# Places of their own for the steps of an attention kernel's head, and other load orders around it

## The chip, the core and the metric

The kernel runs on one core of one Trainium2 chip. The metric is device time in microseconds (us) of one execution, the median of several. Engines are named as the profile names them: PE (TensorE, matmuls), PEld (its weight loads), DVE (VectorE), ACT (ScalarE), POOL (GpSimd), SP (SyncE, which issues almost all DMA transfers here).

## What is computed

Agent attention of four batches, followed by a feed-forward block with a maximum of three products ("maxout"). Cut to what matters:

```python
# q, k, v: (4, 12544, 128); agents: (4, 49, 128)
a2k     = softmax(scale * agents @ k.T)      # over the 12544 keys
agent_v = a2k @ v                            # (49, 128) for each batch
q2a     = softmax(scale * q @ agents.T)      # over the 49 agents
x       = (q2a @ agent_v).reshape(50176, 128)
h       = maximum(maximum(x @ w1, x @ w2), x @ w3)   # 768 columns
out     = h @ w_out                          # (50176, 128)
```

The softmax divides by the sum of exponentials, and the division can be put off to the very end, because the maximum of three linear maps scales with its input.

## The kernel before

**What it makes of the formulas.** For each batch the keys give 49 agent values, `av`. The kernel never forms x. It multiplies `av` by weight *differences* once for each batch: `wall` holds w2 - w1 (columns C21), w3 - w1 (columns C31; in block 4, `FI`, w3 - w2 instead) and linear columns (C1O: w1 times w_out, with zeros on both sides), and `G` is `av` times `wall`. Then for each group of queries: e = exp(scores); u = G[C31] times e, a = ReLU(u), v = G[C21] times e, r = max(v, a); the output is the linear part, e times G[C1O], plus the sum over six blocks of r times w_out, and last a scaling by 1/sum(e). In block 4 ReLU is applied to u in place, v is added onto it in PSUM, and ACT takes the second ReLU.

**Groups.** The 98 row tiles of 128 of a batch are cut into query groups of 8 (49 groups in all; the last takes the remainders of the four batches) and key groups of 9 (11 for a batch). A group has 6 blocks; each costs PE two matmuls for u and two for v (L662), ACT one 128x1024 ReLU (L677), DVE one 128x1024 maximum (L687), and PE eight output matmuls (L701). Two output halves are scaled by DVE (L708) and stored.

**Three parts.** In the head (function `head`) all keys and values of batch 0 are loaded and used, group by group, since G of batch 0 needs them all. In the body, each group of queries carries along one key group of the next batch (`k_group`), and at a batch's end `k_tail` makes the next G. The last batch's groups carry no keys.

**What sets the order.** Nothing is scheduled by dependencies: every step is recorded with a number by `at(key, fn)`, all are sorted by that number, and each engine executes its own steps in that order, waiting where data or a buffer isn't there yet. One query group is 6.0 units. The numbers come from tables: `KEY` for the steady state, `LATE` for groups of the last batch, `OWN` for groups 0, 1, 34 to 37, 47 and 48, `BORDER` for the groups around a change of batch, `BATCH0` and `BATCH3` for `k_tail`. A group's steps: `ld` load of queries, `qc` cast (POOL), `qt` turn (PE), `qe` copy out of PSUM (DVE), `s` scores (PE), `ex` exp (ACT), `sum` and `rec` sums and their reciprocals, `u0` to `u5`, `a0`, `v0`, `x0` and so on for the blocks (x is the maximum), `lin0`, `oc00` and so on for the output, `sc0`, `sc1` scaling, `st` store. Steps in the head have numbers counted from z, the place of the last key group, written as literals (lines 464 to 475).

**Queues and buffers.** All loads and stores stand in SP's one line. A load into the pool `loads` (14 buffers of 576 KB, tag st) is issued when its buffer is free and when the transfer eight before it has landed. PSUM has three buffers of two banks (tag uv) for turns, products and hidden blocks, and two of one bank (tag om) for scores, sums and outputs. Of `a_sb` there are three.

**Steps that the change and the prediction touch.** `load_w(i)` (line 264) loads w1, w2 or w3 as a whole; w1 and w3 are issued before the last values but one, query group 0 after these, w2 after the last values. `cast_w1` (ACT) and `turn_w1` (PE, then a DVE copy into `w1T`) prepare the linear columns. `differences_31`, `difference_f` and `differences_21` (lines 297 to 306) make `wall`; of w2 - w1 DVE takes the first 384 columns and POOL the other 384. `recip` and `normalise` make avT from the sums. `product(c0, on_vector)` (line 412) multiplies avT by 768 columns of `wall` into PSUM (L485) and copies them into G in two pieces, of 256 and 512 columns, on ACT (C31, L420) or DVE (C21, L418), directly after it. `warm(n)` issues n matmuls whose result isn't used (L328), twelve of them (`LAST_WARM`) after the last sums; `keep_busy` issues 32 such small matmuls, in pairs (L788), where groups -2 and -1 would have had their output matmuls. `load_w_out`, `cast_w_out`, `prep_linear` and `acc["lin"]` (lines 778 to 781) have places outside `head`.

Of the kernel before, what the change touches and what calls it, by code (L numbers as in the profile page):

```python
# [28 lines left out]
    "s": -2.94209, "ex": -2.10461, "u1": -0.58526, "a1": -0.11108, "u2": 2.13391, "a2": 3.22306,  # L29
    "v1": 3.39126, "u3": 3.76716, "x1": 4.61365, "v2": 4.65907, "u0": 4.68062, "a3": 4.76358,  # L30
    "x2": 4.9054, "a0": 5.15584, "v0": 5.44974, "u4": 5.62746, "x0": 6.09964, "a4": 6.12388,
    "u5": 6.27862, "v3": 6.63325, "a5": 6.82242, "v4": 6.98304, "x4": 6.98433, "lin1": 7.02719,
    "oc12": 7.03328, "sum": 7.23728, "oc10": 7.59283, "x3": 7.74792, "v5": 7.87225, "rec": 8.46283,
    "x5": 9.47889, "oc13": 9.6877, "oc11": 9.69832, "oc14": 10.58762, "oc15": 10.856, "lin0": 10.87306,
    "oc05": 11.17012, "sc1": 11.55345, "oc01": 11.72189, "oc00": 11.77009, "oc03": 11.79963,
    "oc02": 11.90624, "oc04": 11.95959, "sc0": 12.74339, "st": 15.47059,
# [3 lines left out]
        "u2": 0.64554, "u0": 0.6497, "a0": 0.75101, "a2": 0.92875, "sum": 1.27525, "u3": 2.06003,  # L40
        "v0": 2.59116, "x0": 2.68446, "a3": 2.85638, "rec": 2.96325, "u1": 3.03882, "v2": 3.6736,
        "u4": 4.24684, "a1": 4.93475, "x2": 5.01871, "v3": 5.81978, "u5": 5.84299, "a4": 5.908,
        "a5": 6.60823, "x3": 6.61479, "v4": 6.9759, "v5": 7.08557, "x4": 7.15158, "v1": 7.27894,
        "x5": 7.66161, "x1": 7.70792, "lin0": 9.14279, "oc05": 10.43605, "oc00": 10.7932, "oc02": 10.85481,
        "oc03": 11.37967, "oc01": 11.41219, "oc04": 11.66746, "sc0": 11.83826, "lin1": 12.49398,
        "oc10": 12.50239, "oc11": 12.59233, "oc12": 12.77266, "oc13": 12.88978, "oc14": 13.54796,
        "oc15": 13.60373, "sc1": 13.75975, "st": 20.17439,
    },
    1: {
        "qt": -4.60541, "qe": -4.48042, "s": -2.95099, "ex": -1.32724, "ks": 1.62294, "u0": 1.73602,  # L50
        "ke": 2.36058, "sum": 2.56616, "kv": 2.79082, "a0": 2.92319, "ka": 3.26757, "u2": 3.4201,
        "v0": 3.45964, "a2": 3.84717, "u3": 4.22117, "rec": 4.22129, "x0": 4.49406, "a3": 4.56793,
        "u1": 4.62522, "v2": 4.63012, "x2": 4.73195, "a1": 4.86854, "v3": 5.12545, "u4": 5.25359,
        "x3": 5.55542, "ea": 5.62671, "a4": 5.96399, "u5": 6.17953, "a5": 6.26476, "v1": 6.28947,
        "x1": 6.30399, "v4": 6.40498, "v5": 6.63853, "x5": 6.88027, "x4": 7.41578, "lin0": 8.99321,
        "oc00": 9.79175, "oc04": 10.56667, "oc02": 10.75084, "oc03": 11.28772, "oc01": 11.5494,
        "oc05": 11.68913, "sc0": 12.27589, "lin1": 12.53566, "oc13": 12.60573, "oc15": 12.61178,
        "oc10": 12.70709, "oc14": 13.24775, "oc12": 13.54581, "oc11": 13.80424, "sc1": 14.02652,
        "st": 19.02898,
    },  # L60
    34: {
        "qt": -2.58866, "qe": -1.82932, "s": -1.30778, "ex": -1.10174, "ks": 0.14415, "sum": 0.55608,
        "rec": 0.59015, "ke": 0.68278, "u0": 0.7058, "ea": 0.72143, "u2": 1.49989, "a0": 2.15219,
        "v0": 2.18384, "x0": 2.25012, "kv": 2.57078, "a2": 2.84672, "ka": 3.10787, "u3": 3.14749,
        "a3": 3.82134, "u1": 3.94172, "v3": 3.96473, "a1": 4.22804, "x3": 4.34837, "v2": 4.43956,
        "u4": 4.5536, "u5": 4.96643, "a4": 5.32988, "x2": 5.54314, "a5": 6.22364, "v4": 6.22498,
        "v1": 6.372, "x4": 6.51691, "v5": 6.61382, "x1": 6.73976, "x5": 6.95861, "lin1": 8.28778,
        "oc15": 8.36021, "lin0": 8.73553, "oc13": 9.18722, "oc04": 9.72211, "oc14": 10.51955,
        "oc01": 10.73827, "oc02": 10.8464, "oc03": 12.33286, "oc05": 12.39876, "oc00": 12.40014,
        "oc11": 12.72237, "sc0": 13.30654, "oc12": 14.30997, "oc10": 14.62572, "sc1": 14.9543,  # L70
        "st": 25.03309,
    },
    35: {
        "qt": -2.43671, "qe": -1.9414, "s": -1.5744, "ex": -1.28805, "ks": -1.09088, "ke": -0.64495,
        "sum": -0.18909, "kv": -0.10783, "ka": 0.5331, "rec": 0.56684, "u0": 0.82589, "a0": 0.91902,
        "u2": 1.00358, "v0": 1.49877, "x0": 1.58537, "a2": 2.26288, "u3": 2.5102, "v2": 2.57899,
        "x2": 3.98475, "u1": 4.05488, "a3": 4.05504, "v3": 4.37636, "a1": 4.49639, "u5": 4.62208,
        "x3": 4.92789, "a5": 5.44572, "v5": 5.48263, "x5": 5.93851, "u4": 7.30642, "a4": 8.24488,
        "v1": 8.30836, "x1": 8.49394, "lin0": 8.71742, "oc03": 8.91263, "oc02": 9.07857, "v4": 9.24912,
        "x4": 9.32541, "oc00": 9.39236, "oc04": 9.69131, "oc01": 10.88106, "lin1": 10.92225,  # L80
        "oc05": 11.01981, "oc15": 11.13488, "sc0": 11.61665, "oc12": 11.69455, "oc13": 11.87736,
        "oc14": 13.32657, "oc10": 13.37252, "oc11": 13.49981, "sc1": 13.74093, "st": 42.57773,
    },
    36: {
        "s": -4.45673, "ex": -3.49789, "u1": -0.09348, "a1": 2.12897, "u2": 2.20348, "a2": 2.77677,
        "v2": 3.2876, "u0": 3.526, "v1": 3.8727, "x2": 4.34512, "x1": 4.34975, "u3": 4.36198,
        "a0": 4.73186, "a3": 5.00514, "v0": 5.29756, "u4": 5.75498, "x0": 5.91535, "sum": 6.0162,
        "a4": 6.30588, "v3": 6.39331, "x3": 6.48929, "u5": 6.75132, "rec": 7.30888, "a5": 7.33831,
        "v4": 7.78698, "v5": 7.80684, "x5": 7.96407, "x4": 8.12232, "lin1": 9.0675, "oc12": 9.24639,
        "oc14": 9.95322, "oc10": 10.40131, "lin0": 10.43281, "oc04": 10.55626, "oc01": 10.64608,  # L90
        "oc11": 11.24862, "oc15": 12.02168, "oc13": 12.20592, "oc00": 12.38398, "oc03": 12.91102,
        "sc1": 12.98528, "oc02": 14.0029, "oc05": 14.08645, "sc0": 14.96085, "st": 29.7755,
    },
    37: {
        "s": -2.47874, "ex": -1.87009, "u1": -0.70419, "a1": -0.60046, "u2": 2.0221, "a2": 2.21078,
        "v2": 3.56807, "x2": 3.92118, "u0": 4.2218, "v1": 4.32407, "x1": 4.92454, "a0": 5.43373,
        "v0": 5.83985, "u3": 6.06605, "x0": 6.29959, "u5": 6.46966, "v3": 6.48031, "a3": 6.91113,
        "a5": 7.46701, "u4": 7.96938, "sum": 8.00459, "x3": 8.25588, "rec": 8.25634, "v5": 8.35007,
# [82 lines left out]
def kernel(  # L181
# [18 lines left out]
    nc = tc.nc  # L200
# [4 lines left out]
    P = 128  # L205
# [532 lines left out]

    HEAD_END = KEY["u0"] - 0.01
    Z = NK + 2 + 3.98
    LEAD = 11.0
    HELD = 7
# [90 lines left out]
```

## Time and profile before

| | |
|---|---|
| median of the runs shown | 454.57 us (6 runs, 453.64 to 455.82) |
| the profiled execution, its time | 455.46 us |
| its span, first to last instruction | 453.7 us |
| busy, PE / DVE / ACT / POOL | 434.1 / 404.5 / 398.2 / 169.7 us (96, 89, 88, 37%) |
| PE busy in 0 to 10, 10 to 20, 20 to 30, 30 to 40 us | 2.62, 8.47, 9.02, 8.73 us |
| PE busy in 40 to 44, 44 to 48, 48 to 52, 52 to 56 us | 2.10, 3.97, 3.58, 3.92 us |
| granted clock in 40 to 44, 44 to 48, 48 to 52 us | 0.93, 0.64, 1.00 |
| PE busy in 60 to 100, 100 to 200, 200 to 280 us | 40.00, 99.70, 79.63 us |
| moved by DMA in 10 to 40 us | 408 to 411 GB/s |

The span begins with the head, some 40 us in which keys and values of batch 0 arrive, and then goes over into the body, in which PE is hardly ever idle. The "busy" of an engine is the time in which it executes something; a PE matmul's end is modelled, so a busy PE need not be at its peak. The granted clock is the share of TensorE's full clock. Rows of the timeline that the prediction shows give start (us), busy time (us), engine, line, operation, output, inputs, shapes and, in brackets, how long the engine sat idle before and what ended that.

### The profile page before, as it was taken

What the parts mean: (1) busy time and instruction counts of PE and PEld (TensorE: products, weight loads), DVE (VectorE), ACT (ScalarE), POOL (GpSimd) and SP (SyncE); (2) the same over time, 40 slices, a digit from 0 to 9 for tenths busy, and PEclk for the clock granted to TensorE, in tenths of its full rate; (3) what the DMA queues carried; (4) which work ended last, traced back from release to release, by engine and by line L of the source; (5) the groups of instructions that cost most, each with busy time, mean ns of one, the idle gap of its engine ahead of it and who ended that gap; (6) DMA issues with size and microseconds to landing.
All of it is one profiled execution on the core that took longest, in us unless ns stands there. A gap on an engine that the chain in (4) does not pass through costs nothing.

```text
span 453.7 us, 13313 instructions
## 1 busy us (share of the span) xinstructions
PE 434.1 (96%) x5506; PEld 279.2 (62%) x5506; DVE 404.5 (89%) x505; ACT 398.2 (88%) x456; POOL 169.7 (37%) x165
## 2 busy tenths in 40 slices
PE   2988999999999999999999999999999999999995
PEld 2854566666665666666665666666665556565664
DVE  3323899999999999999999999999999999999995
ACT  1655899999999999999998999999989899999983
POOL 4334465556324454455423354644410101101000
PEclk9999999999999999999999999999999999999999
DMA  8999899997879999998799999999567586566833
GB/s 317 411 410 320 282 290 270 263 298 235 229 242 318 290 300 285 285 325 274 238 309 264 292 330 277 311 322 282 181 208 173 179 196 174 168 183 132 337 140 140
DMA packets 83655, 118.86 MB, mean 262 GB/s; under 512 B 57671, under 2 KB 59659, under 8 KB 83595
## 3 DMA queue, kind: packets, MB, share of 16 engines
q1 hardware_dynamic: 83392, 117.92, 86.4%
q8 instruction: 43, 0.70, 0.6%
q14 instruction: 17, 0.14, 0.1%
q10 hardware_dynamic: 203, 0.10, 0.1%
HBM read 78.74 MB, written 25.69 MB: 230 GB/s over the span
## 4 chain that ended last, share of the span: by engine, by line
PE 86%; DMA 7%; DVE 4%; ACT 1%; issue 1%; SPq 0%; DVEq 0%
PE uv_ps L662 34%; PE o_ps L701 32%; PE o_ps L692 6%; DMA st<-in_v_dram 5%; PE m_ps L639 3%; PE m_ps L625 3%; DVE r L687 2%; PE m_ps L514 2%; PE m_ps L354 2%; DMA st<-in_k_dram 1%; PE uv_ps L328 1%; PE m_ps L650 1%; PE uv_ps L485 1%; DVE o_sb L708 1%; PE o_ps L788 0%
## 5 line engine op out<-in xcount | busy, mean ns | idle before, releaser
L687 DVE TENSOR_TENSOR r<-uv_ps,a_sb 128x1024 bf16<-128x1024 f32 x245 | 297.4, 1222 | 10.1 <-PE uv_ps L662 5.1
L677 ACT ACTIVATE a_sb<-uv_ps 128x1024 bf16<-128x1024 f32 x245 | 242.9, 1024 | 20.2 <-PE uv_ps L662 17.1
L662 PE MATMUL uv_ps<-e_q,G 49*128 49x512 bf16 (+1 forms) x1248 | 182.5, 369 | 2.4 <-ACT G L420 1.0
L701 PE MATMUL o_ps<-wo_bf,r 128*128 128x128 bf16 x2352 | 179.0, 220 | 0.0
L701 PEld LDWEIGHTS <-r 128*128 128x128 bf16 x2352 | 139.8, 98 | 45.2 <-issue 42.1
L662 PEld LDWEIGHTS <-G 49*128 49x128 bf16 x1248 | 57.1, 93 | 63.1 <-issue 25.1
L620 POOL CAST q_bf<-st 128x1024 bf16<-128x1024 f32 x49 | 51.1, 1043 | 98.6 <-DMA st<-in_q_dram 80.7
L708 DVE TENSOR_TENSOR o_sb<-o_ps,recips 128x512 f32<-128x512 f32 x98 | 66.9, 684 | 2.9 <-PE o_ps L701 1.5
L498 POOL CAST v_bf<-st 128x1152 bf16<-128x1152 f32 (+1 forms) x33 | 37.6, 1140 | 49.2 <-DMA st<-in_v_dram 46.9
L494 POOL CAST k_bf<-st 128x1152 bf16<-128x1152 f32 (+1 forms) x33 | 37.6, 1139 | 37.9 <-DMA st<-in_k_dram 37.8
L685 ACT ACTIVATE r<-uv_ps 128x1024 bf16<-128x1024 f32 x49 | 50.2, 1025 | 1.3 <-PE uv_ps L662 0.6
L674 ACT ACTIVATE uv_ps<-uv_ps 128x1024 f32<-128x1024 f32 x49 | 49.5, 1011 | 0.9 <-PE uv_ps L662 0.6
L526 POOL TENSOR_TENSOR Eacc<-Eacc,e_k 128x441 f32<-128x441 f32 x27 | 27.7, 1027 | 39.1 <-ACT e_k L359 38.9
L692 PE MATMUL o_ps<-G,e_q 128*128 128x256 bf16 x196 | 37.9, 274 | 0.0
L645 ACT ACTIVATE e_q<-m_ps 128x512 bf16<-128x512 f32 x49 | 29.2, 596 | 2.3 <-PE m_ps L639 1.2
L629 DVE COPY qT<-m_ps 128x1024 bf16<-128x1024 bf16 x34 | 23.3, 686 | 3.2 <-PE m_ps L625 3.2
L368 DVE COPY kT<-uv_ps 128x1152 bf16<-128x1152 bf16 (+1 forms) x11 | 8.3, 751 | 17.7 <-PE uv_ps L365 17.7
L692 PEld LDWEIGHTS <-e_q 128*128 128x128 bf16 x196 | 12.1, 97 | 18.3 <-issue 18.1
L625 PE MATMUL m_ps<-ident,q_bf 128*128 128x128 bf16 x272 | 21.1, 221 | 0.0
L639 PE MATMUL m_ps<-qT,agT 128*64 128x512 bf16 (+1 forms) x104 | 19.9, 389 | 0.6 <-DVE qT L629 0.6
L383 ACT ACTIVATE v_bf<-st 128x1152 bf16<-128x1152 f32 (+1 forms) x11 | 12.2, 1111 | 8.6 <-DMA st<-in_v_dram 8.6
L378 POOL CAST k_bf<-st 128x1152 bf16<-128x1152 f32 (+1 forms) x11 | 12.5, 1139 | 18.1 <-DMA st<-in_k_dram 18.1
(73 smaller groups left out, 233.4 us busy)
## 6 DMA issues: line engine op xcount, KB each, us to landing
st<-in_q_dram SPq DMA_DIRECT2D x48, 512.0 KB, 5.6
out_dram<-o_sb SPq DMA_DIRECT2D x48, 512.0 KB, 5.3
st<-in_k_dram SPq DMA_DIRECT2D x40, 576.0 KB, 5.5
st<-in_v_dram SPq DMA_DIRECT2D x40, 576.0 KB, 8.8
st<-in_k_dram SPq DMA_DIRECT2D x4, 512.0 KB, 3.8
st<-in_v_dram SPq DMA_DIRECT2D x4, 512.0 KB, 6.6
st<-in_moe_w_dram SPq DMA_DIRECT2D x3, 384.0 KB, 10.7
kT<-k_bf SPq DMA_TRANSPOSE x33, 3.9
```

Of the source, the lines that this page charges most:

```text
L494: nc.gpsimd.tensor_copy(out=d["kb"][:, :n, :], in_=d["k"][:, :n, :])
L498: nc.gpsimd.tensor_copy(out=d["vb"][:, :n, :], in_=d["v"][:, :n, :])
L620: nc.gpsimd.tensor_copy(out=d["qb"], in_=d["q"])
L625: nc.tensor.transpose(t[:, j * P:(j + 1) * P], d["qb"][:, j, :], ident)
L662: nc.tensor.matmul(t[:, h, j0 * P:j1 * P], G[b][h * H:h * H + A, col + f * P:col + (f + 1) * P], d["e"][h * H:h * H + A, j0 * P:j1 * P], s ...
L674: nc.scalar.activation(u, u, AF.Relu)
L677: nc.scalar.activation(a_sb[f], u, AF.Relu)
L685: nc.scalar.activation(r, v_ps[f], AF.Relu)
L687: nc.vector.tensor_tensor(out=r, in0=v_ps[f], in1=a_sb[f], op=ALU.max)
L692: nc.tensor.matmul(t[:, i * 2 * C:(i + 1) * 2 * C], d["e"][:, jj * P:(jj + 1) * P], G[batch[jj]][:, C1O:C1O + 2 * C], start=(i == 0), stop ...
L701: nc.tensor.matmul(t[:, c:c + C], r_sb[f][:, h, jj * P:(jj + 1) * P], wo_bf[:, f, :], start=False, stop=True, skip_group_check=True)
L708: nc.vector.tensor_tensor(out=d["out"][:, j:j + m, :], in0=d["o", o].rearrange("p (j c) -> p j c", c=C), in1=d["r"][:, j:j + m].unsqueeze( ...
```

## The change

It has five parts.

1. The steps of the head get a table `HEAD` with a place for each, in the place of literals. The two copies of each product into G become steps of their own (`evacuate`), and so do the loads of w1, w3 and w2, the load and the cast of w_out, `prep_linear` and `product_linear`.
2. w2 is loaded in two column parts, 512 to 767 first, then 0 to 511. w1 and the queries of group 0 are loaded among the first keys; w3 and the parts of w2 after the last values.
3. Of w2 - w1 nothing is done on POOL any more: `difference_21` does columns 0 to 511 and 512 to 767 on DVE.
4. Group 0's steps from load to exp get places early in the head (`OWN[0]`), `warm(LAST_WARM)` lies further ahead, `turn_w1` behind the products.
5. All tables but `KEY` have new numbers; in `k_tail` the copies of the products have places of their own, and the one on ACT is cut into 512 and 512 columns.

```diff
+HEAD = {
+    "wl0": -11.09161, "wrm": -1.98468, "wl2": 0.51177, "wl1": 0.69065, "wl1b": 0.76707, "w1c": 2.59211,
+    "rcp": 3.16515, "wol": 3.98125, "woc": 4.2069, "d31": 4.34124, "nrm": 4.41073, "df": 4.44324,
+    "p31": 4.74403, "d21a": 4.83164, "e31a": 4.85118, "e31b": 4.89396, "d21b": 5.09254, "p21": 5.48697,
+    "e21a": 6.03394, "e21b": 6.34709, "w1t": 6.98386, "pli": 11.47293, "lin": 11.9489,
+}
 OWN = {
     0: {
-        "u2": 0.64554, "u0": 0.6497, "a0": 0.75101, "a2": 0.92875, "sum": 1.27525, "u3": 2.06003,
+        "ld": -15.45285, "qc": -11.81581, "qt": -10.757, "qe": -10.20555, "s": -9.36462,
+        "ex": -8.65857, "sum": -2.73814, "rec": 0.66113, "u0": 1.73303, "a0": 3.02721, "u3": 3.08353,
...
 BATCH0 = {
-    "red": -0.0796, "tot": 0.34012, "nrm": 0.77389, "p31": 0.90693, "p21": 1.22633,
+    "red": -0.90326, "tot": 0.17632, "nrm": 0.85576, "p31": 0.89274, "e31a": 0.96694, "p21": 1.05183,
+    "e31b": 1.11618, "e21": 1.96962,
 }
...
-    def load_w(i):
-        wst[i] = load_tile().rearrange("p j c -> p (j c)")[:, :Dff]
-        nc.sync.dma_start(wst[i], (moe_w1, moe_w2, moe_w3)[i])
+    def load_w(i, c0=0, c1=Dff):
+        if i not in wst:
+            wst[i] = load_tile().rearrange("p j c -> p (j c)")[:, :Dff]
+        nc.sync.dma_start(wst[i][:, c0:c1], (moe_w1, moe_w2, moe_w3)[i][:, c0:c1])
...
-    def differences_21():
-        difference(nc.vector, C21, 1, 0, slice(0, Dff // 2))
-        difference(nc.gpsimd, C21, 1, 0, slice(Dff // 2, Dff))
+    def difference_21(cols):
+        difference(nc.vector, C21, 1, 0, cols)
...
+        def product(c0):
+            acc[c0] = uv_tile()
+            g_product(acc[c0], acc["av"], c0, c0 + Dff)
+
+        def evacuate(c0, a, z):
+            src = acc[c0].rearrange("p i c -> p (i c)")[:, a:z]
+            if c0 == C21:
+                nc.vector.tensor_copy(out=G[0][:, c0 + a:c0 + z], in_=src)
+            else:
+                nc.scalar.activation(G[0][:, c0 + a:c0 + z], src, AF.Copy)
...
-        at(z + 2.25, cast_w1)
-        at(z + 2.62, turn_w1)
-        at(z + 2.5, differences_31)
-        at(z + 2.65, recip)
-        at(z + 2.66, lambda: warm(LAST_WARM))
-        at(z + 3.91, difference_f)
-        at(z + 3.95, normalise)
-        at(z + 3.955, differences_21)
-        at(z + 3.96, lambda: product(C31, False))
-        at(z + 3.97, lambda: product(C21, True))
-        acc["lin"] = product_linear
+        at(z + HEAD["wl0"], lambda: load_w(0))
+        at(z + HEAD["wl2"], lambda: load_w(2))
+        at(z + HEAD["wl1"], lambda: load_w(1, FI * P, Dff))
+        at(z + HEAD["wl1b"], lambda: load_w(1, 0, FI * P))
...
+        at(z + HEAD["d21a"], lambda: difference_21(LO))
+        at(z + HEAD["d21b"], lambda: difference_21(slice(FI * P, Dff)))
+        at(z + HEAD["p31"], lambda: product(C31))
+        at(z + HEAD["e31a"], lambda: evacuate(C31, 0, 2 * P))
+        at(z + HEAD["e31b"], lambda: evacuate(C31, 2 * P, Dff))
...
-        at(key + keys["p31"], lambda: product(C31, WC, False))
-        at(key + keys["p21"], lambda: product(C21, C31, True))
+        at(key + keys["p31"], lambda: product(C31, WC))
+        at(key + keys["e31a"], lambda: evacuate(C31, 0, FI * P))
+        at(key + keys["e31b"], lambda: evacuate(C31, FI * P, WC - C31))
+        at(key + keys["p21"], lambda: product(C21, C31))
+        at(key + keys["e21"], lambda: evacuate(C21, 0, Dff))
```

In the built program the transfers of the head then stand on SP in this order (k and v with the number of their key group): k0, queries 0, k1, w1, k2, k3, v0, k4, v1, k5, v2, k6, v3, k7, v4, k8, v5, k9, v6, k10, v7, v8, v9, v10, w3, w2 (columns 512 to 767), w2 (0 to 511), and then the body's: k0 of batch 1, queries 1, w_out, v0 of batch 1. Before it was: k0 to k3, v0, k4, v1, and on in turn to k9, v6, k10, v7, v8, w1, w3, v9, queries 0, v10, w2; k0 of batch 1, queries 1, v0 of batch 1, and w_out behind the first turn by DMA.

## The prediction

> **What bounds the kernel now.** I read the chain of waits first, then busy time in windows, then the timeline of the join between head and body. The chain says that TensorE sets the end:
>
> ```profile
> PE 86%; DMA 7%; DVE 4%; ACT 1%; issue 1%; SPq 0%; DVEq 0%
> ```
>
> Read with the windows: from 56 to 445 us PE is busy but for about 1 us. One part of the change touches this body little. Its period stays 8.15 us a group with keys and 7.71 us without (distance between the score matmuls of following groups), as long as the order within a group keeps its number of changes between tile shapes: four L662 cost 0.54 us and two cost 0.32, so 0.11 us goes at every change. I counted the changes in the two built programs: 584 before, 590 after, of which +7 fall in groups 0 and 1, where PE waits anyway, -6 in groups 34 to 38, +4 in the two batch borders. Nothing is left: 0.1 us.
>
> So the question is the join. Up to 40.6 us the loads set the pace (DMA share 1.0); PE is saturated from 54.20 us, the first L692 of group 0. Between lie 13.6 us:
>
> ```profile
> 38.28 1.04 POOL L620 CAST q_bf<-st 128x1024 bf16<-128x1024 f32 x1 [6.35 <-DMA st<-in_q_dram]
> 39.61 0.63 ACT L383 ACTIVATE v_bf<-st 128x512 bf16<-128x512 f32 x1 [1.45 <-DMA st<-in_v_dram]
> 40.04 0.69 DVE L629 COPY qT<-m_ps 128x1024 bf16<-128x1024 bf16 x1 [2.31 <-PE m_ps L625]
> 40.57 0.99 POOL L294 TENSOR_TENSOR wall<-st 128x384 bf16<-128x384 f32 x1 [0.28 <-DMA st<-in_moe_w_dram]
> 40.65 1.06 DVE L294 TENSOR_TENSOR wall<-st 128x128 bf16<-128x128 f32 x1
> 41.63 0.20 DVE L409 TENSOR_TENSOR avT<-m_ps,k_recip 128x49 bf16<-128x49 f32 x1
> ...
> 41.88 0.52 PE L485 MATMUL uv_ps<-wall,avT 128*64 128x512 bf16 x4 [0.38 <-DVE avT L409]
> 42.44 0.87 ACT L420 ACTIVATE G<-uv_ps 128x256 bf16<-128x256 f32 x2 [0.61 <-PE uv_ps L485]
> 43.37 1.01 PE L662 MATMUL uv_ps<-e_q,G 49*128 49x512 bf16 x4 [0.97 <-ACT G L420]
> 44.31 0.85 PE L485 MATMUL uv_ps<-wall,avT 128*64 128x512 bf16 x4
> 45.20 1.02 DVE L418 CAST G<-uv_ps 128x256 bf16<-128x256 f32 x2 [2.90 <-PE uv_ps L485]
> 47.74 1.23 DVE L687 TENSOR_TENSOR r<-uv_ps,a_sb 128x1024 bf16<-128x1024 f32 x1
> ```
>
> The reader is to see three delays: the last values (41.13) stand behind group 0's scores, whose queries landed at 38.28; avT stands behind a 128-column difference that took 1.06 us; the first maximum starts only at 47.74.
>
> **Loads.** Landings are spaced 1.43 us for 576 KB: a full pipe of some 412 GB/s. So landings follow from bytes. Through the second matrix of weights (moe_w2) both versions move the same bytes, and before it landed at 40.57. Counting back: the two column parts land at 40.57 (512 columns) and 39.93 (256), moe_w3 at 39.6, v10 at 38.65 (before 39.6), v9 at 37.4, k10 at 33.1 (before 30.8). The extra transfer costs 0.33 us of SP, hidden since eight loads are out. Query 0 and moe_w1 go ahead of the keys; their 2.2 us delay k10, whose chain (cast 1.04, turn 0.6, copy 0.69, scores 0.4, exp 0.5) ends by 37.7, before v10's cast: hidden. If that cover went, each us would count in full.
>
> **Head, up to the first product.** Removed from PE's line between 39.4 and 41.1: group 0's turn, copy, scores and exp, done some 25 us earlier where PE waits for loads. On POOL its cast (1.04) goes ahead of k2's, which itself lands 2.2 us later: hidden. Group 0's sums and reciprocal (0.20) go ahead of the differences on VectorE, done by 39.5. ACT: v9's cast ends at 38.85, the w1 cast (0.83) now stands before v10's half, so that ends at 39.7+0.63=40.3 although v10 lands 1 us sooner; the other half, on POOL, ends at 39.3. Values to 40.65. Moved onto the path: the two w3-w1 differences, done at 35.65 before, now wait for 39.6 and take 0.89: 40.54. Then avT (0.20) to 40.95, the w2 block difference to 41.25, at its undisturbed row of 0.28. PE's eight fillers (0.45) end at 41.1, the product runs 41.1 to 41.6 (before 41.88 to 42.40): **0.8 us gained**.
>
> [...] The row: a 384-column difference from 41.75 overlapped that cast, took 0.54 as expected, and the cast took 1.25 instead of 1.15. VectorE came first there as it will after; I take 0, and keep 0 to 0.6 for the range.
>
> **Ramp.** Before, the first hidden product asks for columns of the second evacuation; after, u0 needs only the first (0.39): PE starts at 42.05, before at 43.37. The second product follows u0 and the differences: 42.35 to 42.9, its two copies (1.02) end at 43.9 (before 46.2). u0's ReLU 42.6 to 43.6, v0 43.6 to 43.9, first maximum at 44.0 (before 47.74). Added behind it on VectorE: w1T's copy, 0.56 (from 36.80, where it was hidden), and group 1's qT, 0.69. ACT then runs through: a0, a3, a1, a2, a4 to 47.7, exp 48.3, r4 and a5 50.3, e_k 50.8, wall 51.1, group 1's a0 52.1, linear part of G 52.5. VectorE: qT ends at 47.0, x3, x2, x1, x5 at 1.14 to 1.23 each with 0.2 of waiting, 52.2 (before 54.75). PE's linear output starts at 52.55, before at 54.20, **1.65 sooner**, and PE has by then issued two more hidden pairs net, at 0.22: 0.45. **Sum 2.1 us**; ACT and VectorE are some 2.5 ahead, so PE is what binds. Late next is ACT's line to the linear part. w_out lands before group 1's values now, at about 44.3 against a cast at 49.46 before: hidden.
>
> **Tail and borders.** After the last hidden product 40 output matmuls remain in both; both scales and stores come last in both: 0, with 0.1 for one more change of shape. Splitting the border evacuations adds 0.17 on ACT each (385+591 ns in two against 1.02 for about as much), beside PE work. The second border is 0.5 us longer than its work before, so it could gain 0.5 or, with moved products, lose as much; I take 0.
>
> The profiled execution is 455.46 us (span 453.70 and 1.76 around it). Less 2.1: 453.4. The median of the runs shown is 454.57; the same step from it gives **452.5 us**.
>
> **Rivals.**
>
> *Half clock in the new ramp.* These windows are 3.41 us each; the column after the x-counts is the granted clock:
>
> ```profile
> 36.63:40.04 3.41, 3.37 (x31) 1.71 (x29) 0.93 (x2) 1.60 (x2) 1.41 (x2) 1.00 1.03 409
> 40.04:43.45 3.41, 1.51 (x24) 0.79 (x22) 2.25 (x4) 1.67 (x4) 2.65 (x4) 1.00 0.74 297
> 43.45:46.86 3.41, 3.41 (x27) 1.96 (x28) 1.02 (x2) 1.94 (x2) 1.98 (x2) 0.50 0.80 95
> 46.86:50.27 3.41, 3.03 (x30) 1.54 (x28) 3.12 (x4) 2.78 (x4) 0.81 (x1) 1.00 1.01 347
> ```
>
> A window with PE busy 1.51 of 3.41 us was followed by one at 0.50. [...] The row decides: a window of 44% was enough, one of 67% (29.81 to 33.22) was not. The change moves the twelve warming matmuls some 10 us earlier. I count 2.4 to 2.5 us of PE work in the windows 36.6 to 40.0 and 40.0 to 43.5, 70%, so the clock should hold; with other window borders (39 to 42.4) it is 1.75, about 51%. Then products, v0 and turns run at half speed, 0.3+0.2+0.5: gain 1.1, **453.5 us**.
>
> *Given back.* The join gains, but a border or the groups 34 to 37 stall by 1.5 to 2: 454.4. For it: all their places are new. Against: the periodic late order differs by a few outputs only.
>
> *Slower: moe_w3 lands late.* It had 4 us to spare before its use; now none. It is issued behind v10 on SP, waits for a buffer and a landing eight back, and moe_w1 holds one of 14 buffers through the head. Every us after 39.6 moves both products: no gain at 41.7, slower by 0.3% from 43.1; with 3.6 us, **456.1 us**. For it: that nothing covers it. Against: at most eight loads are out, plus moe_w1 and two waiting for casts, 11 of 14.
>
> **Chances.** The measurement tells about 0.3%, 1.4 us, from no change. The join as summed 0.54; half clock 0.18, a third of it still faster; given back 0.14; moe_w3 late 0.14, nearly all slower. So faster 0.60, same 0.26, slower 0.14. Range 450.9 to 455.4: the join with 0.5 from a border and more at ACT's line below, half clock and given back above; the likeliest alone 451.3 to 453.2.
>
> **What would show it.** Right: first product at about 41.1, the first maximum near 44.0, linear output near 52.5, late period 7.71, clock 1.0 from 40 to 50. Wrong: v10's cast or w3's landing after 40.5; a VectorE difference over 0.8 us; clock 0.5 anywhere; more than 1.5 us of PE idle after 56 us.

## The result and the profile after

The changed kernel takes **451.91 us** (median of 28 runs, 451.44 to 455.12); the kernel before took 454.83 in the same series (63 runs, 453.64 to 457.58). The ratio is 0.9944, interval 0.9933 to 0.9956: faster by 2.5 us, more than the 0.3% (1.4 us) that can be told from no change. 452.5 had been predicted.

The profiled execution of the changed kernel took 453.89 us (span 452.1, mean granted clock 0.988). It is not a typical one: 22 of its 28 executions had a clock of 0.997 or more and a median of 451.89; three had 0.988 and took 453.89 to 454.57 (four more took 453.8 to 455.1 at 0.997 or more). The profiled execution of before had lost some clock too (0.996). So this section reads the traces, and the times are read from all the runs.

The chain of waits of the changed kernel, and TensorE's clock in 40 slices of the span:

```profile
PEclk9988899999999999999999999999999999999999
PE 90%; DMA 4%; DVE 3%; ACT 1%; issue 1%; SPq 0%; DVEq 0%; ACTq 0%
```

The three digits 8 are two losses of clock: one from 21.7 to 25.2 us, in the head, and one from 42.2 to 49.0 us, both at a granted 0.50. PE's share of the chain is 90% where it was 86% in before, that of the transfers 4% for 7%. This is no gain of the change: body_old below, with the same head at full clock, has 86 and 5%. In this execution, with the clock lost at 21.7 us, the chain runs through PE from 21 to 37 us, but the first product comes no later for it (40.86 us here, 40.82 in body_old).

The timeline of the join, the same stretch that the prediction showed of before:

```profile
39.42 0.62 ACT L394 ACTIVATE v_bf<-st 128x512 bf16<-128x512 f32 x1
39.74 0.83 DVE L306 TENSOR_TENSOR wall<-st 128x512 bf16<-128x512 f32 x2
...
40.52 0.21 DVE L420 TENSOR_TENSOR avT<-m_ps,k_recip 128x49 bf16<-128x49 f32 x1
40.64 1.22 DVE L306 TENSOR_TENSOR wall<-st 128x128 bf16<-128x128 f32 x3
40.86 0.52 PE L505 MATMUL uv_ps<-wall,avT 128*64 128x512 bf16 x4
...
42.17 0.84 PE L505 MATMUL uv_ps<-wall,avT 128*64 128x512 bf16 x4
...
44.26 1.22 DVE L712 TENSOR_TENSOR r<-uv_ps,a_sb 128x1024 bf16<-128x1024 f32 x1 [0.18 <-PE uv_ps L687]
...
54.24 0.39 PE L717 MATMUL o_ps<-G,e_q 128*128 128x256 bf16 x2
```

The reader is to see that all went by the plan up to 42.2 us. The three differences on VectorE (the block, then 512 and 256 columns) take 1.22 us together, PE has the first product at 40.86 instead of 41.88 and the first maximum (L712) comes at 44.26 instead of 47.74. But the second product takes 0.84 us for the 0.52 of the first, and the linear output comes at 54.24, where before it came at 54.20. The windows of 3.4 us say why (the column after the x-counts is the granted clock):

```profile
38.80:42.20 3.40, 2.02 (x33) 1.30 (x34) 2.57 (x8) 2.03 (x4) 0.58 (x2) 1.00 1.05 382
42.20:45.60 3.40, 3.40 (x21) 1.39 (x20) 2.31 (x4) 2.95 (x4) 2.03 (x2) 0.50 1.03 258
45.60:49.00 3.40, 3.40 (x24) 1.51 (x21) 1.17 (x2) 2.15 (x3) 1.92 (x2) 0.50 1.18 201
```

Two windows at half clock followed one in which PE was busy for 2.02 us. In the profiled execution of before one window was at half clock.

Behind the join, the time from the scores of group 2 to PE's last output is 391.25 us in before (57.46 to 448.71) and 390.27 in after (56.76 to 447.03). So 1.0 us was won in a part in which the prediction saw nothing.

### The profile page after: what moved, and what is told of

Read it like the earlier page. It is cut to its first block, busy times and chain, and to the rows that moved or that the text cites. A ratio compares the mean times of both kernels' runs of the same rounds, so it can differ in the third digit from the quotient of the medians.

```text
span 452.1 us, 13320 instructions
## 1 busy us (share of the span) xinstructions
PE 434.1 (96%) x5506; PEld 278.1 (62%) x5506; DVE 403.8 (89%) x506; ACT 398.3 (88%) x459; POOL 168.7 (37%) x164
## 4 chain that ended last, share of the span: by engine, by line
PE 90%; DMA 4%; DVE 3%; ACT 1%; issue 1%; SPq 0%; DVEq 0%; ACTq 0%
PE uv_ps L687 35%; PE o_ps L726 31%; PE o_ps L717 6%; PE m_ps L650 4%; PE m_ps L664 3%; DMA st<-in_v_dram 3%; PE m_ps L534 2%; DVE r L712 2%; PE uv_ps L339 2%; PE m_ps L365 2%; DMA st<-in_k_dram 1%; PE m_ps L675 1%; PE uv_ps L505 1%; PE uv_ps L376 1%; DVE o_sb L733 1%; PE o_ps L809 1%
## 5 line engine op out<-in xcount | busy, mean ns | idle before, releaser
L712 DVE TENSOR_TENSOR r<-uv_ps,a_sb 128x1024 bf16<-128x1024 f32 x245 | 297.5, 1222 | 9.7 <-PE uv_ps L687 5.1
L726 PE MATMUL o_ps<-wo_bf,r 128*128 128x128 bf16 x2352 | 176.1, 220 | 0.0
L650 PE MATMUL m_ps<-ident,q_bf 128*128 128x128 bf16 x272 | 21.7, 225 | 0.0
L370 ACT ACTIVATE e_k<-m_ps 128x441 bf16<-128x441 f32 (+1 forms) x33 | 17.8, 539 | 2.1 <-PE m_ps L675 0.7
```

The source lines that it names most:

```text
L650: nc.tensor.transpose(t[:, j * P:(j + 1) * P], d["qb"][:, j, :], ident)
L712: nc.vector.tensor_tensor(out=r, in0=v_ps[f], in1=a_sb[f], op=ALU.max)
L726: nc.tensor.matmul(t[:, c:c + C], r_sb[f][:, h, jj * P:(jj + 1) * P], wo_bf[:, f, :], start=False, stop=True, skip_group_check=True)
```

## The experiments

The theory after the result: the join is what gains most, the body brings about 1 us of its own, and the clock decides how much of the join is kept. All kernels ran in four sets, each on another chip and beside the kernel before (454.48, 455.04, 455.40 and 454.57 us, medians in the four sets). All results are in one table; the last two columns split a kernel's executions by granted clock.

| kernel | median us | ratio to before, interval | at 0.997 or more: runs, median | below 0.993: runs, median |
|---|---|---|---|---|
| after | 451.91 | 0.9944, 0.9933 to 0.9956 | 22 of 28, 451.89 | 3, 453.93 |
| body_old | 453.08 | 0.9953, 0.9936 to 0.9971 | 9 of 16, 453.02 | 2, 454.98 |
| join_old | 455.62 | 1.0012, 0.9993 to 1.0030 | 0 of 14 | 12, 455.62 |
| pool_diff | 460.96 | 1.0120, 1.0084 to 1.0157 | 0 of 6 | 6, 460.96 |
| group0_late | 452.44 | 0.9954, 0.9937 to 0.9971 | 17 of 21, 452.37 | 3, 455.69 |
| pool_diff2 | 453.65 | 0.9968, 0.9942 to 0.9993 | 6 of 12, 452.88 | 5, 455.23 |
| loads_old | 455.52 | 0.9982, 0.9955 to 1.0008 | 3 of 12, 452.25 | 9, 455.58 |
| warm4 | 452.03 | 0.9937, 0.9915 to 0.9960 | 8 of 12, 451.88 | none |
| body_new | 454.05 | 0.9981, 0.9961 to 1.0001 | 9 of 12, 453.82 | none |
| loads_old_warm4 | 453.22 | 0.9976, 0.9946 to 1.0006 | 6 of 12, 452.67 | 1, 457.50 |
| before_warm4 | 455.43 | 0.9998, 0.9983 to 1.0013 | 12 of 12, 455.44 | none |
| border_old | 453.69 | 0.9969, 0.9949 to 0.9989 | 8 of 12, 453.50 | 1, 456.05 |
| border12_old | 453.51 | 0.9980, 0.9962 to 0.9999 | 5 of 12, 452.76 | 5, 455.28 |

The kernel before has 454.3 to 454.5 at 0.997 or more (73 of 125 executions in the four sets), and medians of 455.3 to 455.8 at 0.993 to 0.997 (37); the other 15 lie below and are slower still.

### body_old: all of the head, nothing of the body

```diff
-LATE, OWN[34] to OWN[48], BORDER, BATCH0, BATCH3: the numbers of after
+LATE, OWN[34] to OWN[48], BORDER, BATCH0, BATCH3: the numbers of before
-        at(key + keys["e21"], lambda: evacuate(C21, 0, Dff))
+        at(key + keys["p21"], lambda: evacuate(C21, 0, Dff))
```

(and the copy on ACT whole, directly behind its product)

> The changed kernel with all tables of the body as they were before (LATE, OWN of groups 34 to 48, BORDER, BATCH0, BATCH3, and each border's product copied out at once). Theory 'the gain is made in the join': the same time as the changed kernel, 451.9 us within 0.5, and in the profile the first linear output of group 0 as early as with the change. Rival 'the body's new places bring a good part': 453 us or more. Rival 'given back': faster than the changed kernel by over 0.5, 451.4 or less.

It took 453.08, 1.2 us more than after (1.1 at full clock): behind the new head the body is worth about that. The head alone is worth 1.3 us, 453.02 against 454.29 of before, both at full clock in the same set. Its profiled execution kept a clock of 0.999, so it shows the new join undisturbed; its timeline (L982 is the product, L1188 the maximum, L1193 the linear output, L1140 the scores, of group 2 in the last row):

```profile
39.39 0.62 ACT L871 ACTIVATE v_bf<-st 128x512 bf16<-128x512 f32 x1
40.82 0.52 PE L982 MATMUL uv_ps<-wall,avT 128*64 128x512 bf16 x4
42.14 0.52 PE L982 MATMUL uv_ps<-wall,avT 128*64 128x512 bf16 x4
43.82 1.22 DVE L1188 TENSOR_TENSOR r<-uv_ps,a_sb 128x1024 bf16<-128x1024 f32 x1
51.80 0.39 PE L1193 MATMUL o_ps<-G,e_q 128*128 128x256 bf16 x2
54.31 0.41 PE L1140 MATMUL m_ps<-qT,agT 128*64 128x512 bf16 x2
```

First and second product, first maximum and linear output stand 0.2 to 0.3 us (the last 0.75) ahead of the places that the prediction gave them: 41.1, 42.35, 44.0, 52.55.

### body_new: the head of before, the body of after

```diff
-LATE, OWN[34] to OWN[48], BORDER, BATCH0, BATCH3: the numbers of before
+LATE, OWN[34] to OWN[48], BORDER, BATCH0, BATCH3: the numbers of after
-        at(key + keys["p21"], lambda: product(C21, C31, True))
+        at(key + keys["p21"], lambda: product(C21, C31))
+        at(key + keys["e21"], lambda: evacuate(C21, 0, Dff))
```

> The kernel before, with only the body's places from after (the last groups, both borders, groups 34 and on), the head as before. Theory: the body's places are worth 1.0 us by themselves, as body_old showed from the other side: 453.2 to 453.7. Rival: they pay only behind the new join: 454.2 to 454.8. The prediction's value for this kernel is no change from the kernel before.

454.05, in between the two expectations, and the interval of its ratio reaches 1. Among executions of full clock it took 453.82 against 454.47 of before in the same set: 0.65 us for the body by itself. With this body the new head is worth 1.9 us (451.89 in after, though from another set). Its trace runs from group 2's scores to PE's last output in 390.24 us, as after does. Its head is that of before at a clock of 0.998, which the profile of before could not show (L974, L1181, L1186 and L1133 answer to the rows above):

```profile
40.05 0.63 ACT L872 ACTIVATE v_bf<-st 128x512 bf16<-128x512 f32 x1 [1.45 <-DMA st<-in_v_dram]
42.33 0.52 PE L974 MATMUL uv_ps<-wall,avT 128*64 128x512 bf16 x4 [0.38 <-DVE avT L898]
44.35 0.52 PE L974 MATMUL uv_ps<-wall,avT 128*64 128x512 bf16 x4
46.74 1.23 DVE L1181 TENSOR_TENSOR r<-uv_ps,a_sb 128x1024 bf16<-128x1024 f32 x1
53.20 0.38 PE L1186 MATMUL o_ps<-G,e_q 128*128 128x256 bf16 x2
56.45 0.41 PE L1133 MATMUL m_ps<-qT,agT 128*64 128x512 bf16 x2
```

Group 2 begins at 56.45 with the old head and at 54.31 with the new one, both at full clock: 2.1 us. Part of that is that this execution's last values came late (their cast at 40.05; 39.61 in the profile of before). Counted from that cast it is 16.40 us against 14.92: 1.5. So the join is worth 1.5 to 2.1 us in the traces, and 1.3 (with the old body) to 1.9 (with the new one) in the medians of full clock.

### border_old and border12_old: where the body's gain lies

border_old takes BORDER, BATCH0 and BATCH3 from before and copies each product at once. The last batch's division then stands ahead of the addition of its last values (0.578 against 0.599 in group 35), so these are left out of its sums; the work is otherwise the same.

> After with the borders' places alone from before (both tails of the keys, the groups beside the borders, each copy of a border's product at once behind it); groups 34 and on and the head stay. body_old lost 1.1 to 1.2 us of medians for all of the body. If the second border carries it (its four groups took 34.90 us before, 34.29 in after): 452.4 to 453.0. If single longer groups elsewhere carry it (8.50 for 8.15 us at three places before, at one in after): 451.7 to 452.1.

453.69, outside both expectations, 1.8 more than after and worse than body_old: here the third border mixes places of before with those of after. The next version therefore takes the first two borders alone:

```diff
-BORDER, BATCH0: the numbers of after
+BORDER, BATCH0: the numbers of before, each product of these two tails copied at once
```

> After with the places of the first and second border alone from before (groups beside them, the keys' tails, each copy of a product at once behind it); the third border, groups 34 and on and the head stay. In the traces the second border's four groups took 34.29 us in after and in body_new, 34.90 to 35.01 in the kernels with the old places, and single groups of 8.50 us instead of 8.15 came back at two places behind the first border with them. If the places of these two borders carry the body's gain: 0.6 for the border and 0.35 for each longer group that comes back, median 452.6 to 453.4. If they do not: 451.7 to 452.2.

453.51, just above the expected 452.6 to 453.4; seven of twelve had lost clock. At full clock it is 452.76, 0.9 more than after. The timeline's score matmuls of the groups around the second border, in after and then in border12_old, show the first part of it:

```profile
221.56 0.41 PE L664 MATMUL m_ps<-qT,agT 128*64 128x512 bf16 x2
...
237.44 0.41 PE L664 MATMUL m_ps<-qT,agT 128*64 128x512 bf16 x2
247.45 0.41 PE L664 MATMUL m_ps<-qT,agT 128*64 128x512 bf16 x2
255.85 0.41 PE L664 MATMUL m_ps<-qT,agT 128*64 128x512 bf16 x2
```

```profile
222.11 0.41 PE L817 MATMUL m_ps<-qT,agT 128*64 128x512 bf16 x2
...
238.07 0.41 PE L817 MATMUL m_ps<-qT,agT 128*64 128x512 bf16 x2
248.54 0.41 PE L817 MATMUL m_ps<-qT,agT 128*64 128x512 bf16 x2
256.97 0.41 PE L817 MATMUL m_ps<-qT,agT 128*64 128x512 bf16 x2
```

The four groups take 255.85 - 221.56 = 34.29 us with the new places and 34.86 with the old: 0.57, most of it in the group that carries the border (10.01 against 10.47). The second part: two groups outside the borders take 8.50 us instead of 8.15 in border12_old, as in before and body_old; after and body_new have neither, but one of 8.06 to 8.07 instead of 7.71 near 380 us. Sum: 0.57 + 2 x 0.35 - 0.35 = 0.9.

The 0.57 is not all the order of the border. In its long group a VectorE maximum begins late, with no releaser that the profile shows. The first row is of before, the second of pool_diff2 (next section), whose body has all the numbers of after:

```profile
246.91 1.23 DVE L687 TENSOR_TENSOR r<-uv_ps,a_sb 128x1024 bf16<-128x1024 f32 x1 [0.25 <-issue]
243.87 1.23 DVE L712 TENSOR_TENSOR r<-uv_ps,a_sb 128x1024 bf16<-128x1024 f32 x1 [0.27 <-issue]
```

In after this maximum follows without a gap. pool_diff2 takes 10.37 us for the group and 34.65 for the four, 0.35 more than after with the same numbers. So the order of the border is worth some 0.2 us, and the rest of the 0.9 is longer groups.

### pool_diff and pool_diff2: half of w2 - w1 on GpSimd again

```diff
-        at(z + HEAD["d21a"], lambda: difference_21(LO))
-        at(z + HEAD["d21b"], lambda: difference_21(slice(FI * P, Dff)))
+        at(z + HEAD["d21a"], lambda: difference_21(nc.vector, slice(0, Dff // 2)))
+        at(z + HEAD["d21b"], lambda: difference_21(nc.gpsimd, slice(Dff // 2, Dff)))
```

> The changed kernel, with columns 384 to 767 of w2 - w1 on GpSimd again and 0 to 383 on VectorE. Theory 'the two exclude each other': the 128-column difference takes about 1.0 us instead of 0.28, the first product's second half and both its copies come 0.5 to 0.8 us later, 452.6 us. Rival 'ACT's line hides it, or GpSimd's half gains it back for the second product': 451.9 us within 0.3.

Both numbers of the first theory are from before, where one 128-column difference took 1.06 us while GpSimd's half (0.99) ran, and the other, with GpSimd idle, 0.28.

460.96, and neither theory was tested: the place of `d21b` lies behind casts for the body in GpSimd's one line. The timeline shows GpSimd's half and the product that waits for it:

```profile
47.77 0.99 POOL L306 TENSOR_TENSOR wall<-st 128x384 bf16<-128x384 f32 x1
48.81 0.85 PE L505 MATMUL uv_ps<-wall,avT 128*64 128x512 bf16 x4 [6.50 <-POOL wall L306]
```

So pool_diff2 gives GpSimd's half the place z + 3.95, ahead of these casts.

> As pool_diff, with GpSimd's half of the w2 differences given its place ahead of GpSimd's cast of the next keys, so that it starts when w2 has landed (40.6 us). Contention theory: it reads SBUF while VectorE runs the 128-column differences of two float32 SBUF inputs, and one of the two holds the other up: the three blocks take about 1.06 us as in the kernel before (0.28 in after), the first product starts 0.8 us later, and the median is 452.5 to 452.9. If the engines do not hold each other up: the blocks stay at 0.28 us, GpSimd's half is done by 41.7, and the median is 451.6 to 452.2.

453.65, and 452.88 at full clock: 1.0 more than after. At full clock the size is as expected, the place is not. VectorE began the block 0.08 us before GpSimd began (40.33 and 40.41), and the block took its 0.28; it was VectorE's own 384 columns that took longer. The answer for the line of the differences (the numbers are least, median and longest in ns):

```profile
L306 DVE TENSOR_TENSOR wall<-st x4: 281/460/1349, 39.4 to 40.5; 128x128 bf16<-128x128 f32 x2, 128x512 bf16<-128x512 f32 x1, 128x384 bf16<-128x384 f32 x1
L306 POOL TENSOR_TENSOR wall<-st x1: 1055/1055/1055, 40.4 to 40.4; 128x384 bf16<-128x384 f32 x1
```

The 384 columns took 1.35 us where the same difference took 0.54 in before, and ended 0.4 us after GpSimd's half. Yet from avT to the second product it is 1.82 us here and 1.65 in after, and group 2 begins at 54.20 against 54.31 in body_old: in this execution the join lost nothing by it. What it lost is in the body: three groups are 0.36 us longer (8.51 and 8.50 for 8.15, 10.37 for 10.01 at the second border), though no number of the body was changed. The chain of waits in the first of them:

```profile
116.57 0.77 PE uv_ps L687 x6
117.34 0.24 issue
117.58 1.24 DVE r L712
118.82 0.04 issue
118.86 0.39 PE uv_ps L687 x2
```

PE waits for a maximum that began 0.36 us later in the period than in the group before (109.07 there, 8.51 us earlier for a period of 8.15). The longer groups of before and body_old show the same pieces. They go with the program and not with one execution: pool_diff, on another chip, has the same three groups (8.52, 8.50 and 10.37), and join_old, with the same numbers in the body, has none. Counted in VectorE's line of the trace, the three late maxima of pool_diff2 stand 77 instructions apart, those of before 77 and 75. Why it is these places isn't settled.

### join_old: the old places of the join behind the new loads

```diff
-    "w1t": 6.98386, "d31": 4.34124, "rcp": 3.16515, "df": 4.44324, "nrm": 4.41073, "d21a": 4.83164, ...
+    "w1t": 2.62, "d31": 2.5, "rcp": 2.65, "df": 3.91, "nrm": 3.95, "d21a": 3.955, ...
```

(group 0 from behind its exponentials on and all of group 1, too)

> The changed kernel's loads, early queries of group 0, VectorE-only differences and body, but the join's steps (differences, products, copies, blocks of groups 0 and 1, linear part) at the places of before. Theory 'the places make the gain': the w3-w1 differences now stand ahead of the sums' reciprocal and avT on VectorE and wait for w3 at 39.6, so the first product starts at about 42 and the time is that of before within 0.6, 454.3 us. Rival 'loads and early queries make it': 452.5 us or less.

455.62, no gain left and 1.3 more than expected; none of its 14 executions had full clock. In its trace the first product begins at 42.66 (41.88 in before) and group 2 at 58.57 (57.46), so with the old places the earlier loads and queries bring nothing at the join. Its timeline shows GpSimd's key cast beside VectorE's differences, for which the prediction took 0:

```profile
42.52 1.96 DVE L618 TENSOR_TENSOR wall<-st 128x512 bf16<-128x512 f32 x2
42.53 1.68 POOL L826 CAST k_bf<-st 128x1152 bf16<-128x1152 f32 x1 [2.80 <-DMA st<-in_k_dram]
45.11 0.18 PEld L817 LDWEIGHTS <-avT 128*64 128x64 bf16 x4 [0.83 <-DVE wall L618]
```

VectorE began first, by 0.01 us. The two pieces of w2 - w1 then took 1.96 us together: 0.68 for the 512 columns and 1.365 for the 256, which take 0.42 in after. The key cast took 1.68 us for the 1.15 in after and ended at 44.21; that it came in between the pieces is read from these times and not shown. PE did not pay for it here: the last piece ended at 44.48, while PE was busy with the first hidden product from 44.15 to 45.18, so the 0.83 in brackets is idle time of its weight loads alone. The second product begins 2.45 us after the first, in before 2.43. In after both pieces end at 41.86, 0.18 us before that cast; as its second product begins at 42.17, a last piece 0.9 us longer would cost up to 0.6 there (an estimate from these figures).

### group0_late: the queries of group 0 after the last values but one

```diff
-        "ld": -15.45285, "qc": -11.81581, "qt": -10.757, "qe": -10.20555, "s": -9.36462, "ex": -8.65857,
```

> The changed kernel, with the load, cast, turn, copy, scores and exp of query group 0 where they were (load between the last two loads of values, the rest ahead of the last values), its sums behind the second product. Theory 'each part of the join's chain counts little by itself, since VectorE's differences end as late': 0.2 to 0.5 us slower than the changed kernel, 452.3 us. Rival 'the early queries are the gain': 453.5 us or more.

452.44, close to the expected 452.3: 0.5 us more than after, and the same at full clock (452.37 against 451.89). The early scores bring that much and no more.

### loads_old and the fillers: what the clock is worth

```diff
-    "wl0": -11.09161, "wl2": 0.51177, "wl1": 0.69065,
+    "wl0": -0.9, "wl2": -0.8, "wl1": 0.35,
-        at(z + HEAD["wl1"], lambda: load_w(1, FI * P, Dff))
-        at(z + HEAD["wl1b"], lambda: load_w(1, 0, FI * P))
+        at(z + HEAD["wl1"], lambda: load_w(1))
```

> After, with w1 and w3 loaded again before the last two value loads and w2 whole behind them; the early queries and all places stay. Theory of landings (the prediction's): the last values land at 39.6 instead of 38.65, ScalarE's half of their cast ends about 0.3 to 0.9 us later, and all of the join with it: median 452.2 to 452.8. Rival: the join waits for w1 and w2 as long as for the values, and the order brings nothing: 451.7 to 452.1.

455.52: far outside both expectations. Three executions at full clock have a median of 452.25, in the expected size; nine of twelve lost clock and took 455.58. The windows of its trace:

```profile
39.00:42.50 3.50, 1.71 (x31) 1.21 (x31) 2.57 (x8) 2.13 (x5) 1.06 (x2) 1.00 1.06 381
42.50:46.00 3.50, 3.50 (x19) 1.25 (x20) 2.13 (x3) 3.03 (x4) 1.97 (x2) 0.53 0.90 241
46.00:49.50 3.50, 3.50 (x26) 1.75 (x23) 1.22 (x3) 2.39 (x3) 1.92 (x2) 0.50 1.26 230
```

PE is busy 1.71 us of the 3.5 ahead of the join (2.02 of 3.4 in after), and some 7 us at half clock follow. It also has the key cast beside VectorE's pieces, with another outcome than join_old:

```profile
41.26 1.22 DVE L323 TENSOR_TENSOR wall<-st 128x128 bf16<-128x128 f32 x3
42.05 1.43 POOL L530 CAST k_bf<-st 128x1152 bf16<-128x1152 f32 x1 [1.79 <-DMA st<-in_k_dram]
```

The three pieces take 1.22 us as in after; here it is the cast that takes longer, 1.43 us for 1.15. It came 0.09 us before the end of the 512 columns, in join_old at their start.

To test the clock, PE was given work ahead of the join:

```diff
+        at(z + 3.4, lambda: warm(4))
         at(z + HEAD["df"], difference_f)
```

(four 512-column products between the products of the last two value tiles; in warm4 on after, in loads_old_warm4 on loads_old, in before_warm4 on before)

> After, with four more filling 512-column products between the products of the last two value tiles (0.85 us of TensorE work where it would be idle). Theory: the half clock in some executions comes from the 3.4 us in which TensorE is busy only 2.0 us; with 2.8 busy it goes, no execution lies near 453.9, and the median is 451.5 to 451.9. Rival: the clock is lost elsewhere or by chance: still about a quarter of the executions above 452.7 and the same median; if the products delay the last values, 452.2 to 452.8.

> loads_old with the four filling 512-column products of warm4 between the products of the last two value tiles. In loads_old nine of twelve executions had a granted clock of 0.991 or less and lay at 454.9 to 456.5, three had 0.999 and lay at 452.1 to 452.6. Clock theory: the longer idle time before the join is what loses the clock; with it filled, most executions keep 0.995 or more and the median is 452.2 to 452.8. Rival: the order of loads itself costs the 3 us (the later landing, or transfers in each other's way): 455.0 to 455.8 as in loads_old.

> The kernel before with the same four filling products between its last two value tiles. In the second set of runs 19 of its 35 executions lay at 453.6 to 455.0 with a clock of 0.998 or more, the others at 455.3 to 458.4 with 0.996 or less. Clock theory: the second kind goes; median 454.0 to 454.5, hardly an execution above 455.2. Rival: its half clock comes after the stretch behind the last values (41 to 44 us), where nothing is filled: the mixture stays, 454.6 to 455.2.

loads_old_warm4: 453.22, between the two expectations. One execution of twelve is below 0.993 instead of nine, five more lie at 0.993 to 0.996. The same stretch of its trace:

```profile
39.00:42.50 3.50, 2.52 (x33) 1.43 (x33) 2.18 (x8) 2.13 (x4) 0.67 (x2) 1.00 1.07 378
42.50:46.00 3.50, 2.71 (x26) 1.35 (x27) 2.53 (x5) 3.48 (x5) 2.39 (x2) 1.00 0.75 212
```

So of the 3.6 us by which the median of loads_old stood behind after, 2.3 came back with work that computes nothing. The ratios to before can't tell the two apart (0.9982 and 0.9976, with intervals that overlap), as three of the twelve took over 457 us. That the clock is what costs is seen more clearly within loads_old: 452.25 at full clock, 455.58 without. warm4: none of twelve below 0.993, but after had lost it in three of 28 only, and the medians (452.03 and 451.91) don't differ. Its own profiled execution took 456.43 for another reason: PE waited 1.62 us for a cast of queries and was busy for 1.79 us of the 3.41 before 279.57, and a stretch of half clock followed (six turning matmuls took 0.85 us from 279.76, where eight take 0.61 at 289.19). before_warm4: all twelve at 0.997 or more, as expected, but at 455.44, a miss: here the fillers stand ahead of the product with the last values (42.05 instead of 41.13), the first product begins at 42.73 instead of 41.88, and what the clock gives is lost again.

None of the versions beats after by more than the runs can tell.

## Why the prediction was right, and where it was not

**The bound and the place.** Right for the larger part: 1.3 to 1.9 of the 2.5 us lie between the last loads and group 2, and PE sets the end behind it. The rest lies in the body, where the prediction saw nothing.

**Loads.** The order told from bytes held. In loads_old the last values' cast on ACT begins at 40.05 and in after at 39.42: 0.63 us, where 0.4 came to the time at full clock (three executions).

**Head.** Right: the first product at 40.86 (41.1 predicted), so 1.0 us gained for 0.8, and avT at 40.52 (40.54). moe_w3, the rival on the slower side, landed in time: its differences begin at 39.74 for 39.65.

**GpSimd's cast beside VectorE's pieces.** Taking 0 for the key cast was right for this kernel. The rows of before that it rests on, VectorE's and then GpSimd's:

```profile
41.75 0.54 DVE L294 TENSOR_TENSOR wall<-st 128x384 bf16<-128x384 f32 x1
42.04 1.25 POOL L494 CAST k_bf<-st 128x1152 bf16<-128x1152 f32 x1 [0.48 <-DMA st<-in_k_dram]
```

But the reason given, that VectorE comes first, was too narrow: it came first in join_old too (42.52 and 42.53), and there its last piece took 1.365 us for 0.42. The 0 to 0.6 us that the prediction kept is a term that no run shows: in after the pieces end at 41.86 and the cast begins at 42.04, and in join_old, where they met, PE did not wait for the longer piece. Nor does a run show an end of the differences that gives the 42.35 of the second product; in after they end at 41.86, and it begins at 42.17. What decides which of the two takes longer isn't shown: in join_old the cast began with the first piece and the last piece took longer, in loads_old it began 0.09 us before the end of the 512 columns and the cast took longer (1.43 us).

**Ramp.** The "Sum 2.1 us" of "1.65 sooner" and 0.45 came out smaller in the time: 1.5 to 2.1 in traces of full clock, 1.3 to 1.9 in the medians. The step that failed is the base. The prediction set its new ramp, all at full clock, against rows of a ramp that had itself run at half clock from 43.4 to 46.9. It saw that window and used it for a rival only. body_new shows the old ramp at full clock: its first maximum is 6.69 us after the cast of the last values (46.74 - 40.05), in the profile of before 8.13 (47.74 - 39.61). About 1.4 us of the gain at that point was the clock of one execution, some of which the ramp's later waits absorb. At the linear output the base was 54.20; at full clock it is 53.20, though the last values came 0.44 later. The new ramp was summed too late as well, 52.55 for the 51.80 of body_old, and the two errors partly cancel.

**Body and borders.** "Nothing is left: 0.1 us" and "I take 0" for the second border: the mis-sized term, by 0.6 (body_new) to 1.0 us. The count of shape changes fits the period, which is 8.15 and 7.71 in both, but it says nothing of single groups. The second border gave 0.6 (34.89 to 34.29; "could gain 0.5" was named), 0.35 of it by a maximum that is no longer late, and two groups of 8.50 became regular against one that became longer. As pool_diff2 has three longer groups again with the same numbers, that part of the gain is luck and not the plan of the new places.

**Half clock in the new ramp.** This rival is not what the median shows, but it happened in the profiled execution and, by their clock of 0.988, most likely in two more of 28; "clock 0.5 anywhere" was named as a sign of being wrong. Its price was put at 1.0 us (453.5 for 452.5); it is 2.0 (453.93 against 451.89), and two windows are lost in the trace and not one.

That it could depend on where the windows lie was foreseen, and two traces agree with it; no run tested it by itself. In after the stretches of half clock begin at 21.74, 42.22 and, behind all work, 451.82 us: 20.48 and 409.60 us apart, 6 and 120 times 3.413. The author's estimate takes this for a fixed step and counts back by it from the end of body_old's trace, which gives these windows:

```profile
36.73:40.15 3.42, 2.40 (x51) 1.69 (x50) 0.90 (x3) 3.00 (x5) 0.61 (x1) 1.00 1.04 397
40.15:43.56 3.41, 2.58 (x30) 1.31 (x30) 2.54 (x8) 2.18 (x4) 1.45 (x2) 1.00 1.07 362
```

PE is busy for 2.40 and 2.58 us, about the 2.4 to 2.5 that the prediction had counted, and the clock is 1.00 in both. Between 38.81 and 42.22 in after it is busy for 2.04, and 0.50 follows.

So the sum came out 0.6 us from the measurement because two errors stood against each other: a join that brings 0.2 to 0.8 less and a body that brings 0.6 to 1.0 more. That it came so close is luck.

## What to carry to other kernels

Before a stretch of one trace is used as the base of a difference, look whether its clock was full, and take a second execution or an experiment that keeps it. When every place in a periodic body is new, an equal period is not enough: list the distances group by group, since borders and single longer groups hold what the average hides, and look whether a version with the same numbers has the same longer groups before they are credited to the numbers. And a half operation on an in-order engine needs its place checked against that engine's own line first: one GpSimd step behind the wrong casts cost 9 us here (460.96 in pool_diff, 451.91 in after).

## What the runs showed of the hardware

In the 3.41 us ahead of a half clock PE's longest idle gap was 0.97 us in before (up to 43.37), and in after 1.12 (up to 21.14) and 0.85 (up to 40.10). A stretch at 0.50 lasted 3.41 us in before (43.44 to 46.85), 3.41 (21.74 to 25.15) and 6.83 (42.22 to 49.05) in after and some 10.2 in group0_late (40.82 to 51.06). In the stretches of before and after PE was busy all the time. In the 3.41 us ahead of the stretches at the join it had been busy for 1.51 us (before), 2.04 (after), 1.92 (loads_old), 1.61 (group0_late) and 1.11 (join_old). These shares alone don't tell when the clock goes: body_new kept 1.00 behind 2.10 us in the 4.00 from 40 to 44, and loads_old_warm4 behind at most 1.63 in 3.41, since it stood idle for 1.78 up to 39.88 and had 1.00 from 39.0 to 49.5.

Where one of VectorE's differences (two float32 inputs) and a GpSimd operation overlapped, one of the two often took longer than the same elsewhere: a 128-column difference took 0.28 us when it began 0.08 us ahead of GpSimd in pool_diff2, and 1.06 when it began 0.08 us behind it in before (1.06 in body_new and 1.05 in before_warm4, 0.09 behind). Being first with one instruction did not keep the next from it: of two that followed each other while a GpSimd operation ran, the second took 1.35 us (0.54 in before) in pool_diff2 and 1.365 (0.42 in after) in join_old. In loads_old, where GpSimd's cast began 0.09 us before the end of the 512 columns, the three pieces took 1.22 us together, as in after, and the cast 1.43 for 1.15.
